# Attention and a mixture of experts in one kernel: a shorter distance for routing products, and a seventh block pair

## The chip, the cores and the metric

The kernel runs on one core of a Trainium2 chip. The metric is the device time of one execution in microseconds; the times given are a median of several runs, and beside it one execution taken by the hardware profiler. TensorE multiplies matrices, VectorE (DVE) and ScalarE (ACT) work elementwise, GpSimd (POOL) here issues the transfers that gather and scatter rows by an index, and SyncE (SP) issues plain transfers.

## The reference, cut to what matters

Channel attention over 4 batches of 5056 positions and 256 channels, and behind it a mixture of 8 experts over the 20224 rows that it gives:

```
s = normalised(k).T @ normalised(q) / tau        # 256 x 256 a batch
x = (v @ softmax(s)).reshape(20224, 256)
logits = x @ w_gate                              # 20224 x 8
# all (row, expert) pairs in falling order of their logit: a row goes to the first
# expert that still has room; each expert takes 20224 / 8 = 2528 rows
out[rows of e] = relu(x[rows of e] @ w1[e]) @ w2[e]   # 256 -> 1024 -> 256
```

The assignment depends on all logits, so the kernel finds it expert by expert: it searches the threshold above which the next full expert takes its rows, takes these rows out, and goes on with the experts that are left.

## The kernel before, in words

**Order of the work.** First attention and the gate (to about 319 us of the span), then the experts in the order in which they become full. An "expert 5" below is the one that comes sixth (p = 5). Each has 2528 rows, in chunks of up to 512 rows (`CUT`: five chunks, c = 0 to 4). A chunk is gathered from memory by row (`fetch` in `load_x`, line 1490), turned so that the 256 inputs lie on the partitions (`turn`), multiplied by w1 (`layer1`, eight groups of 128 features, six products each), and by w2 (`layer2`, one group of 24 products for each 128 rows), and scattered by row to the output (line 1753).

**Precision.** Every operand is split into a high part, rounded to the format that TensorE takes at full speed, and a low part, the difference. A product is three: high by high, high by low, low by high. ScalarE makes the high parts (copies, or relu for the hidden layer), VectorE the low ones.

**Block pairs.** `MIXED` names, for some experts, the chunks at which a pair of chunks is taken together: the first layer of both is a 2 by 2 by 2 block product, which `layers` (line 1760) forms with seven block products instead of eight. `STEPS` is its order, written out by hand: P1 to P7 are the block products, c.. and p7 copies on ScalarE, j.. joins on VectorE, hi and lo the two parts of the hidden layer. `turn_parts` prepares the chunks of a pair (with more differences and roundings than `turn`), `sums_w` the weights. Before, experts 4 and 5 have one pair (chunks 3 and 4), experts 6 and 7 two (chunks 1 and 2, 3 and 4).

**Routing.** While the experts are computed, the routing of later experts goes on in the gaps: generators (`route`, `compact`) yield the engine and the estimated cost of their next instruction, and the planner `Order` (line 1245) keeps clocks for TensorE (`pe`) and VectorE (`dve`) and puts such an instruction into the engines' queues where its inputs should be there. `hook` does this after each product of the layers. A routing product (engine "P") is put in when the end of its input, `st.ready`, lies `margin` ns behind the clock of TensorE; "q" is a product without that distance. `margin` is 0 in the first part, 150 during expert 0 (`FIRST_MARGIN`) and 700 from expert 1 on (`MARGIN`). The routing of an expert is first a search (rounds that count rows above trial thresholds: L711, L715 and ScalarE's L688, summed by a product at L860 and L873, L725 or L839), then a compaction, which makes the list of rows (products L1073, countings by ScalarE L1135, or by VectorE L1153 and L1158). For experts 6 and 7 the compaction's products, but for the first, are of kind "q" (line 1140). The list is needed when the first chunks of that expert are gathered.

**Held.** While `o.held` is set, `hook` passes over all routing streams. `layers` sets it at every step: always in a pair that begins before chunk 3, always for the last expert, and otherwise once the index list of the next expert is there.

Of the kernel before, what the change touches and what calls it, by code (L numbers as in the profile page):

```python
# [21 lines left out]
E, F = 8, 1024  # L22
# [50 lines left out]
DVE_TO_DVE = 70  # L73
EARLY_GAP = 100
MARGIN = 700
FIRST_MARGIN = 150
TURN_LAT = 1150
LAYER_LAT = 1050
# [14 lines left out]
DEPTH = 4  # L93
PAD_X = 88
PARTED = (4, 5, 6, 7)
MIXED = {4: (3,), 5: (3,), 6: (1, 3), 7: (1, 3)}
LOAD_AT = (1, 0)
GATHER_AT = {1: ("p7.0", "cAB.1", "cBZ.1", "hi12.0", "cAB.2", "p7.2", "hi11.2", "cAB.3"),
             3: ("p7.0", "cAB.1", "cBZ.1", "hi12.0", "hi21.1", "hi11.2", "cBZ.3", "hi11.3",
# [11 lines left out]
def attention_moe(ctx: ExitStack, tc: tile.TileContext, q, k, vt, tau, wg, w1t, w2t, tabs, out):  # L111
# [3 lines left out]
    P = nc.gpsimd  # L115
# [497 lines left out]
    done = {}  # L613
# [628 lines left out]
    class Order:  # L1242
        def __init__(self):
            self.pe = self.dve = self.act = 0.0
            self.margin = 0
            self.patient = self.queued = False
            self.held = self.inner = False
            self.main = []
            self.streams = []

        def add(self, gen, prio):
            st = Stream(gen, prio)
            st.mine = st.ready = max(self.dve, self.pe)
            self.streams.append(st)
            return st

        def scalar(self, at, cost):
            if not self.queued:
# [16 lines left out]
        def hook(self):  # L1275
            moved = True
            while moved:
                moved = False
                best = None
                if self.main:  # L1280
                    best = (max(self.dve, self.main[0][0]) + self.patient * GAP, 0, None)
                for st in () if self.held else list(self.streams):
                    if st.next is None:
                        self.streams.remove(st)
                        continue
                    eng, cost = st.next
                    if eng == "W":
                        st.step()
                        if st.next is None or st.next[0] != "W":
                            moved = True  # L1290
                            break
                    elif eng == "M":
                        st.mine = max(st.mine, cost)
                        st.step()
                        moved = True
                        break
                    elif eng == "A":
                        if st.ready <= self.pe:
                            st.mine = st.ready = self.scalar(self.pe, cost) + ACT_LAT
                            st.step()  # L1300
                            moved = True
                            break
                    elif eng in "Ppq":
                        if eng == "p" or st.ready + (self.margin if eng == "P" else 0) <= self.pe:
                            self.pe += cost
                            st.mine = st.ready = self.pe + PE_TO_DVE
                            st.step()
                            moved = True
                            break
                    else:  # L1310
                        c = (max(self.dve, st.mine) if eng == "V" else self.dve, st.prio(), st)
                        if self.patient and c[1] == EARLY_PRIO:
                            c = (c[0] + EARLY_GAP,) + c[1:]
                        if best is None or c[:2] < best[:2]:
                            best = c
                if moved:
                    continue
                if best is not None and best[0] <= self.pe + SLACK:
                    moved = True
                    if best[2] is None:  # L1320
                        self.run_main()
                    else:
                        st = best[2]
                        self.dve = best[0] + st.next[1]
                        st.mine = self.dve + DVE_TO_DVE
                        st.ready = self.dve + DVE_TO_PE
                        st.step()
# [13 lines left out]
    o = Order()  # L1341
# [127 lines left out]
    def load_x(p, c, paced=False):  # L1469
        idx = routed[p]["src"]  # L1470
# [19 lines left out]
        def fetch(i, col, n, after=None):  # L1490
            at = idx[:n, col:col + 1]
            if paced:
                at = ffx.tile([128, 1], I32, name="pace", bufs=4)[:n]
                S.activation(at, idx[:n, col:col + 1], AF.Copy)
            if by_v and n < 128:
                P.memset(xg[n:128, i], 0.0)
            P.memset(spacer, 0.0)
            got = P.indirect_dma_start(out=xg[:n, i, :], out_offset=None, in_=x_d,  # L1498
                                       in_offset=bass.IndirectOffsetOnAxis(ap=at, axis=0))
            if after is not None:  # L1500
                tc.add_manual_dep(got.ins, after.ins.name, SPACED, reason="room between gathers")
            if i == len(cols) - 1:
# [219 lines left out]
    def layer2(p, c, h, inserts, behind=()):  # L1722
# [4 lines left out]
        idx = routed[p]["idx"]  # L1727
        for i, col in enumerate(cols_of(p, c)):
# [7 lines left out]
            for fbs in [[fb for fb in range(8) if not any(fb in g for g in late)]] + list(late):  # L1736
                for l, w in ((hH, wH), (hH, wL), (hL, wH)) if fbs in late else ((hH, wH), (hL, wH), (hH, wL)):
                    for fb in fbs:
# [8 lines left out]
                        if j % 2 == 0:  # L1747
# [2 lines left out]
            S.activation(y[:n], py[:n, 0:C], AF.Copy)  # L1750
            o.scalar(o.pe + 200, 390)
            P.memset(spacer, 0.0)
            sd = P.indirect_dma_start(out=out, out_offset=bass.IndirectOffsetOnAxis(ap=idx[:n, col:col + 1], axis=0),  # L1753
                                      in_=y[:n], in_offset=None)
            for s_ in scat:
# [4 lines left out]
    def layers(p, c):  # L1760
# [32 lines left out]
            o.dve += 690  # L1793

        for step in STEPS:
            o.held = c < 3 or p == E - 1 or bool(done.get(("idx", p + 1)))
            op, g = step.split(".")
            g = int(g)
            A, D = fresh[g % 2], fresh[1 - g % 2]
# [40 lines left out]
    with tc.manual_schedule():  # L1840
# [62 lines left out]
        for p in range(E):  # L1903
# [80 lines left out]
            if p + 1 in PARTED:  # L1984
                at_end[0] = [cut_more]
                at = LOAD_AT[p in PARTED]
# [67 lines left out]
```

## Time and profile before

| | |
|---|---|
| median of 3 runs | 1251.32 us (1250.91 to 1252.19) |
| the profiled execution, its own time | 1249.44 us |
| its span, first to last instruction | 1247.7 us |
| TensorE busy | 1227.2 us (98%) |
| VectorE busy | 935.2 us (75%) |
| ScalarE busy | 646.6 us (52%) |
| GpSimd busy | 382.3 us (31%) |

Rows name the line of the kernel, the engine, the operation, and the tiles as output<-inputs. Times are from the start of the span, in us; a row of the order of time has start and duration, and in brackets how long the engine stood idle ahead of it and what ended that. The ends of TensorE's products are modelled, so the distance between their starts says more than their durations. The experts begin at 319 (0), 454 (1), 576 (2), 695 (3), 809 (4), 920 (5), 1033 (6) and 1138 us (7).

### The profile page before, as it was taken

To read this page: it belongs to the slowest core of one execution; us is meant where nothing else is said; L and a number is where in the kernel's file an instruction comes from. 1 tells how busy PE (TensorE), PEld (TensorE's weight loads), DVE (VectorE), ACT (ScalarE), POOL (GpSimd) and SP (SyncE) were. 2 spreads that over 40 slices of the span, in tenths; PEclk is the share of its full clock that TensorE was granted. 3 is DMA by queue.
4 is the path that set the end of the run, shared out by engine and by line. 5 is a ranking of instruction groups with operands and counts; after the bars stand their busy time and mean duration, and the time that the engine had idled before them with its cause. 6 is when DMAs were issued, how large, how long until landed. Compare 5 with 4: busy or idle time off the path is not lost.

```text
span 1247.7 us, 23699 instructions
## 1 busy us (share of the span) xinstructions
PE 1227.2 (98%) x8710; PEld 1096.5 (88%) x8710; DVE 935.2 (75%) x2396; ACT 646.6 (52%) x1491; POOL 382.3 (31%) x693
## 2 busy tenths in 40 slices
PE   8999999999999989999999999999999999999998
PEld 7889977898888978899899898988898998989898
DVE  6688597798778767877876987897787777766752
ACT  6646653467324533534542665547654565664652
POOL 0000000001532255144333434333452444444422
PEclk9999999999999999999999999999999999999999
DMA  8899875436232126344624543453454364545410
GB/s 309 308 406 415 323 267 200 157 153 257 60 88 97 49 63 162 101 111 105 168 82 94 134 116 92 111 145 95 104 141 102 101 153 114 117 103 131 106 46 33
DMA packets 223812, 184.62 MB, mean 148 GB/s; under 512 B 152656, under 2 KB 193488, under 8 KB 219088
## 3 DMA queue, kind: packets, MB, share of 16 engines
q1 hardware_dynamic: 196624, 103.66, 29.5%
q0 software_dynamic: 17664, 58.22, 14.7%
q10 hardware_dynamic: 9408, 21.24, 4.4%
q8 instruction: 68, 1.11, 0.4%
q14 instruction: 48, 0.39, 0.1%
HBM read 123.30 MB, written 59.77 MB: 147 GB/s over the span
## 4 chain that ended last, share of the span: by engine, by line
PE 82%; DMA 6%; issue 5%; POOL 2%; DVE 2%; ACT 2%; SPq 0%; POOLq 0%; ACTq 0%; DVEq 0%
PE py L1740 30%; PE ph L1691 24%; PE px L295 8%; PE s L347 8%; PE ph L1779 4%; PE py L1779 3%; DMA x_d<-xs 2%; PE pc L860 2%; DMA ua<-in_q_dram 1%; POOL out_dram L1753 1%; PE px L473 1%; DMA uc<-in_k_dram 1%; PE pi L1073 1%; POOL xg L1498 1%; DMA uc<-in_q_dram 1%
## 5 line engine op out<-in xcount | busy, mean ns | idle before, releaser
L1740 PE MATMUL py<-uc,hH 128*128 128x256 f32 (+1 forms) x2560 | 337.2, 280 | 0.5 <-ACT c L1750 0.3
L1740 PEld LDWEIGHTS py<-uc,hH 128*128 128x128 f32 (+1 forms) x2560 | 314.1, 187 | 2.9 <-ACT c L1750 0.5
L1691 PE MATMUL ph<-xH,ua 128*128 128x512 f32 (+3 forms) x928 | 251.0, 388 | 0.3 <-issue 0.2
L1498 POOL DMA_INDIRECT xg<-x_d,src x156 | 156.1, 1000 | 178.4 <-ACT hH L1694 73.4
L1694 ACT ACTIVATE hH<-ph 128x512 fp32r<-128x512 f32 (+3 forms) x232 | 134.2, 580 | 133.9 <-PE ph L1691 127.2
L1691 PEld LDWEIGHTS ph<-xH,ua 128*128 128x128 f32 x928 | 166.9, 189 | 30.4 <-ACT xH L1656 0.6
L1753 POOL DMA_INDIRECT out_dram<-y,idx x105 | 107.3, 1022 | 269.1 <-ACT y L1750 216.2
L1700 DVE SCALAR_TENSOR_TENSOR hL<-ph,hH 128x512 fp32r<-128x512 f32 (+3 forms) x232 | 153.7, 665 | 42.0 <-ACT hH L1694 36.9
L1740 PE MATMUL py<-uc,hL 128*128 128x256 f32 (+1 forms) x1280 | 181.7, 280 | 0.2 <-issue 0.2
L1740 PEld LDWEIGHTS py<-uc,hL 128*128 128x128 f32 (+1 forms) x1280 | 161.5, 187 | 0.7 <-issue 0.6
L1691 PE MATMUL ph<-xL,ua 128*128 128x512 f32 (+3 forms) x464 | 141.5, 385 | 0.0
L1750 ACT ACTIVATE y<-py 128x256 f32<-128x256 f32 (+1 forms) x105 | 40.2, 383 | 158.1 <-PE py L1740 129.1
L1691 PEld LDWEIGHTS ph<-xL,ua 128*128 128x128 f32 x464 | 85.2, 188 | 15.8
L347 PE MATMUL s<-ua 128*128 128x256 f32 x320 | 73.8, 387 | 3.3 <-DMA ua<-in_q_dram 2.3
L347 PEld LDWEIGHTS s<-ua 128*128 128x128 f32 x320 | 60.9, 193 | 15.4 <-issue 7.4
L298 ACT ACTIVATE xs<-px 128x512 f32<-128x512 f32 (+2 forms) x98 | 49.7, 520 | 47.6 <-PE px L295 45.5
L347 PE MATMUL s<-uc 128*128 128x256 f32 x320 | 71.5, 380 | 0.6 <-DMA uc<-in_q_dram 0.6
L347 PEld LDWEIGHTS s<-uc 128*128 128x128 f32 x320 | 60.2, 190 | 10.1 <-issue 1.6
L295 PE MATMUL px<-aH,vh 128*128 128x256 f32 (+1 forms) x232 | 67.7, 294 | 0.5 <-ACT aH L263 0.5
L295 PE MATMUL px<-aH,vl 128*128 128x256 f32 (+1 forms) x232 | 65.8, 284 | 1.4 <-DVE vl L274 1.4
L295 PE MATMUL px<-aL,vh 128*128 128x256 f32 (+1 forms) x232 | 65.8, 284 | 0.0
L363 DVE TENSOR_TENSOR acc_k<-acc_k,sq 128x1024 f32<-128x1024 f32 x36 | 43.9, 1220 | 19.8 <-ACT sq L362 19.3
(431 smaller groups left out, 2127.9 us busy)
## 6 DMA issues: line engine op xcount, KB each, us to landing
x_d<-xs ACTq DMA_DIRECT2D x39, 512.0 KB
xr<-xg SPq DMA_DIRECT2D x34, 512.0 KB
xq<-xr SPq DMA_DIRECT2D x136, 128.0 KB
vr<-in_vt_dram SPq DMA_DIRECT2D x14, 1024.0 KB
uc<-in_k_dram SPq DMA_DIRECT2D x18, 512.0 KB
uc<-in_q_dram SPq DMA_DIRECT2D x18, 512.0 KB
ua<-in_k_dram SPq DMA_DIRECT2D x17, 512.0 KB
ua<-in_q_dram SPq DMA_DIRECT2D x17, 512.0 KB
```

The costliest lines, as they stand in the source:

```text
L295: mm = PE.matmul(px[:, i * C:i * C + width], lhsT=l_, rhs=a_, start=(j == 0), stop=(j == len(terms) - 1))
L298: S.activation(xs[:, t % TH:t % TH + n, 0:width], px[:, 0:n * width].rearrange("p (t c) -> p t c", t=n), AF.Copy)
L347: newest[0] = PE.matmul(sb[:, ib * C:(ib + 1) * C], lhsT=kt[:, t, ib * 128:(ib + 1) * 128], rhs=qt[:, t, :], start=(first and t == 0 and i ...
L363: V.tensor_tensor(acc, acc, sq, op=OP.add)
L1498: got = P.indirect_dma_start(out=xg[:n, i, :], out_offset=None, in_=x_d, in_offset=bass.IndirectOffsetOnAxis(ap=at, axis=0))
L1691: PE.matmul(ph[:, 0:nt], lhsT=l[:, w], rhs=x_[:, kb, 0:nt], start=(i == 0), stop=(i == 5))
L1694: relu = S.activation(hH[:, fb, 0:nt], ph[:, 0:nt], AF.Relu)
L1700: V.scalar_tensor_tensor(hL[:, fb, 0:nt], ph[:, 0:nt], 0.0, hH[:, fb, 0:nt].bitcast(F32), op0=OP.max, op1=OP.subtract)
L1740: mm = PE.matmul(py[:n, 0:C], lhsT=l[:, fb, tk], rhs=w[:, d], start=(j == 0), stop=(j == 23))
L1750: S.activation(y[:n], py[:n, 0:C], AF.Copy)
L1753: sd = P.indirect_dma_start(out=out, out_offset=bass.IndirectOffsetOnAxis(ap=idx[:n, col:col + 1], axis=0), in_=y[:n], in_offset=None)
L1779: PE.matmul(dst, lhsT=w[b][l][:, f], rhs=x[a][i], start=(first and n == 0), stop=(n == 2), skip_group_check=True)
```

## The change

Three things. `MIXED` gets a second pair for expert 5, chunks 1 and 2, so that expert 5 is worked like expert 6. The planner gets a record of the row transfers: `transfer` is called at each gather and scatter with an estimated start; a transfer that would start less than 1600 ns behind the last one (each takes 1280 ns by the planner's account) marks the next 3500 ns as shaken. `room` gives the distance for routing products: `margin` while shaken, else at most 250 ns. And `o.held` is false in all pairs, so that routing goes on there.

```diff
+QUIET = 250
+POOL_STEP = 1280
+CLOSE = 1600
+SHAKEN = 3500
...
-MIXED = {4: (3,), 5: (3,), 6: (1, 3), 7: (1, 3)}
+MIXED = {4: (3,), 5: (1, 3), 6: (1, 3), 7: (1, 3)}
...
+            self.moved = self.shaken = -1e9
...
+        def transfer(self, at):
+            start = max(at, self.moved + POOL_STEP)
+            if start < self.moved + CLOSE:
+                self.shaken = start + SHAKEN
+            self.moved = start
+
+        def room(self):
+            return self.margin if self.pe < self.shaken else min(self.margin, QUIET)
...
-                        if eng == "p" or st.ready + (self.margin if eng == "P" else 0) <= self.pe:
+                        if eng == "p" or st.ready + (self.room() if eng == "P" else 0) <= self.pe:
...
+            o.transfer(o.pe + 300)
...
+            o.transfer(o.pe + 900)
...
-            o.held = c < 3 or p == E - 1 or bool(done.get(("idx", p + 1)))
+            o.held = False
```

## Rows read from the trace of the kernel before

**Rows 1.** The page: the span, and TensorE's busy time, share and instructions.

```profile
span 1247.7 us, 23699 instructions
PE 1227.2 (98%) x8710; PEld 1096.5 (88%) x8710; DVE 935.2 (75%) x2396; ACT 646.6 (52%) x1491; POOL 382.3 (31%) x693
```

**Rows 2.** Busy time of each engine (instructions), clock, DMA: experts 5 and 6.

```profile
920.10:1033.10 113.00, 111.89 (x758) 101.28 (x757) 86.72 (x221) 63.97 (x172) 46.61 (x85) 1.00 0.47 119
1033.10:1138.10 105.00, 105.00 (x702) 95.56 (x701) 72.69 (x130) 61.52 (x128) 46.42 (x83) 1.00 0.48 119
```

**Rows 3.** Waits of TensorE, 455 to 1138 us: total, times, longest.

```profile
PE pi L1073 <- ACT ext L1137: 1.1, 2, 0.9
PE pc L873 <- DVE Ex L869: 0.6, 1, 0.6
PE pc L725 <- DVE Ec L721: 0.5, 1, 0.5
PE pc L1073 <- DVE G L1064: 0.2, 1, 0.2
```

**Rows 4.** TensorE in order of time, within the pair of expert 4.

```profile
880.70 0.62 PE L1779 MATMUL py<-xH,ua 128*128 128x512 f32 x2
...
881.38 0.62 PE L1779 MATMUL py<-xH,ua 128*128 128x512 f32 x2
```

**Rows 5.** The same table as rows 2: a pair, a plain layer, a pair.

```profile
989.80:1009.20 19.40, 19.40 (x87) 15.66 (x86) 13.44 (x27) 14.49 (x26) 9.33 (x18) 1.00 0.49 116
1033.10:1044.00 10.90, 10.90 (x50) 9.04 (x49) 8.80 (x15) 8.25 (x21) 3.78 (x6) 1.00 0.50 119
...
1055.30:1074.70 19.40, 19.40 (x87) 15.65 (x86) 13.84 (x31) 14.49 (x26) 10.09 (x21) 1.00 0.48 113
```

**Rows 6.** Groups by line: a join and a copy; busy us, mean ns, idle before.

```profile
L1791 DVE TENSOR_TENSOR ph<-ph,p 128x512 f32<-128x512 f32 x24 | 16.6, 692 | 0.0
...
L1787 ACT ACTIVATE p<-py 128x512 f32<-128x512 f32 x24 | 14.4, 601 | 2.6 <-PE py L1779 2.1 <-ACT ph L1787 0.4
```

**Rows 7.** In order of time: routing products, an input of two, three transfers.

```profile
512.89 0.67 PE L860 MATMUL pc<-eq,ge 128*128 128x48 bf16 x20
...
553.37 0.95 POOL L1498 DMA_INDIRECT xg<-x_d,src  x1 [0.28 <-issue]
...
554.62 0.99 POOL L1753 DMA_INDIRECT out_dram<-c,idx  x1 [0.21 <-issue]
...
557.75 0.26 DVE L869 TENSOR_TENSOR Ex<-Dr,jsel 120x96 fp32r<-120x96 f32 x1
...
558.06 0.32 PE L873 MATMUL pc<-Ex,ones_q 128*128 128x96 f32 x1 [0.62 <-DVE Ex L869]
...
679.31 0.19 PE L873 MATMUL pc<-Ex,ones_q 128*128 128x64 f32 x1
...
795.73 0.22 PE L725 MATMUL pc<-Ec,ones_q 128*128 128x12 f32 x1
...
864.62 0.97 POOL L1753 DMA_INDIRECT out_dram<-y,idx  x1 [2.08 <-ACT y L1750]
...
865.16 0.40 DVE L836 CAST Ec<-cnt 128x8 fp32r<-128x8 f32 x1 [1.10 <-ACT junk L688]
...
865.71 0.24 PE L839 MATMUL pc<-Ec,ones_q 128*128 128x8 f32 x1
...
1022.62 0.38 PE L1073 MATMUL pc<-E__108,G 128*128 128x162 bf16 x3 [0.17 <-DVE G L1064]
```

**Rows 8.** Line 836: shortest/median/longest ns, first and last start, shapes.

```profile
L836 DVE CAST Ec<-cnt x10: 157/170/404, 854.1 to 950.2; 128x8 fp32r<-128x8 f32 x8, 128x16 fp32r<-128x16 f32 x2
```

**Rows 9.** The same for the products of lines 839 and 1073.

```profile
L839 PE MATMUL pc<-Ec,ones_q x10: 168/168/244, 854.9 to 951.4; 128*128 128x8 f32 x8, 128*128 128x16 f32 x2
...
L1073 PE MATMUL pi<-E__108,G x144: 230/233/246, 290.3 to 1044.4; 128*128 128x162 bf16 x144
```

**Rows 10.** In order of time: compaction beside the preparation of a pair.

```profile
985.34 0.40 ACT L1135 ACTIVATE junk<-pi,rhalf 128x160 bf16<-128x160 f32 x1
...
985.62 0.21 ACT L1135 ACTIVATION_READ_ACCUMULATOR junk<-pi,rhalf 128x1 f32 x1
985.71 0.18 ACT L1137 ACTIVATE ext<-pi 128x6 f32<-128x6 f32 x1
...
985.95 0.37 PE L1073 MATMUL pi<-E__108,G 128*128 128x162 bf16 x3 [0.94 <-ACT ext L1137]
```

## The prediction

> **What bounds the kernel now.** I read the page first. TensorE is busy for 1227.2 of the 1247.7 us of the span [rows 1], and the table by expert says that this is no average over unlike stages: 111.89 of 113.00 us in expert 5, 105.00 of 105.00 in expert 6, at a granted clock of 1.00, while VectorE has 86.72 and 72.69 us and ScalarE 63.97 and 61.52 us there [rows 2]. So a change is worth what it takes from, or adds to, TensorE's own stream: products fewer, or waits inside the stream. Next the waits of TensorE from expert 1 to the end of expert 6 (455 to 1138 us): 2.4 us in all, each of them a routing product (L1073, L873, L725) that stood at the head of TensorE's queue before its input was there; no row is a wait for a gathered row, a weight load or an index list [rows 3]. So nothing in this stretch waits for the routing to be finished. Routing done sooner buys no time by itself; it can only allow other things.
>
> **The sixth and seventh chunk in a block pair: a gain.** Chunks 1 and 2 of expert 5 go from two plain first layers to one block pair (the seventh pair of the kernel, there are six now). In products this is 96 against 7 x 4 x 3 = 84, so 12 fewer, of 512 columns each. Inside a pair the groups of three start 0.68 us apart (880.70, 881.38), 0.227 us a product [rows 4], so 12 x 0.227 = 2.72 us. The stages say a little less: a plain first layer without routing takes 10.90 us, two 21.80; a pair without routing 19.40, whose first products come slower [rows 5]. The difference, 2.4 us, is what I take; the 2.72 is the upper end. The second layers of both chunks are the same products as before.
>
> The Trainium skill ("TensorE: Matmul & The Clock Gate", Back-to-back issue gap) gives N/2.4 + 2.5 ns for an isolated warm product, 215.8 ns for 512 columns. An estimate by that page would be 12 x 0.2158 = 2.59 us. The trace's 0.227 us is longer and decides.
>
> What the pair adds lies on VectorE and ScalarE: 8 joins of 0.69 us and 12 copies of 0.6 us beyond the plain layers [rows 6], and a preparation with 7 more differences and 3 more roundings, by the same rows some 5 us of VectorE and 2 us of ScalarE. In expert 5 that makes about 97 of 110 us on VectorE and 74 on ScalarE. Expert 6, with the same two pairs, runs at 105.00 of 105.00 us of TensorE [rows 2], so alone this is hidden. The cover is thinner in expert 5, because routing sits there as well; that is the third part.
>
> **A shorter distance for routing products: a loss of about a microsecond.** Until now each routing product of experts 1 to 7 is put into TensorE's queue when the planner's clock is 700 ns past the planned end of its input; it becomes 250 ns unless a close transfer is noted. For expert 0 the distance is 150 already and min(150, 250) leaves it. TensorE runs its queue in order, so a product whose input is late holds every product of the layers behind it, and through them the ScalarE and VectorE work that reads those. I measured how far the input's end lies ahead of the product's start, for the 91 routing products between 455 and 1138 us for which the input can be read off. Most stand 0.7 to 1.5 us off; the floor is about 0.05 us (557.75 + 0.26 to 558.06, where TensorE waited). Whoever is under 0.50 us now would lose up to 0.45 us at the shorter distance. There are thirteen of them; the first is at 512.89, the last at 1022.62 [rows 7]. Counting a transfer as close when its row on GpSimd starts within 1.6 us of the one before, and 3.5 us behind it as shaken, 34 of the 91 are shaken, with nine of the thirteen (the transfers at 553.37 and 554.62 stand ahead of the one at 558.06), and 57 are not, with four (at 512.89, 679.31, 795.73 and 865.71) [rows 7]. So the rule of the change does pick out the risky third: 26% against 7%. The four unshaken have 0.17, 0.35, 0.17 and 0.15 us (the last from 865.16 + 0.40 to 865.71) and would lose 0.33 + 0.16 + 0.34 + 0.36 = 1.2 us. All thirteen, if the planner's guess at the transfers misses the real ones, 4.1 us. The other end is a small gain: where the routing falls elsewhere, today's waits need not return. I take +1.2, the sum over the rows to which the rule applies.
>
> The rows also show what one transfer does to a short operation: the CAST at 865.16 took 0.40 us beside a transfer that began at 864.62, where the median of its line is 170 ns and the longest of ten 404 [rows 7, 8]; that is 0.2 us more. The Trainium skill ("SBUF — State Buffer", Who interferes with whom) says that copies, casts and tensor_scalar can hold the port pair that VectorE shares with GpSimd, that whoever is second is blocked for the whole instruction, and that tensor_reduce never contends. By that rule any transfer disturbs, close or not, but by no more than its own length, and 250 ns would cover the 0.2 us seen; the shorter distance would then cost nothing. The four unshaken steps, 0.8 us and more short of the usual distance, say that something else is late there as well (ScalarE's counting ahead of the CAST, 1.10 us of idle time). The rule is the ground of the first rival below.
>
> **Routing in pairs: about half a microsecond lost.** Today the routing streams stand still in every first pair, in all of expert 7, and in the second pair once the next index list is there. The stages at 989.80 and 1055.30 have 13.44 and 13.84 us of VectorE and 14.49 of ScalarE in 19.40 [rows 5], so 5 to 6 us of either are free. A search round of routing 6 (ten of them, 854.9 to 951.4 [rows 9]) brings 3 countings of 0.6 us on ScalarE, a compaction of 6 or 7 twelve more. The planner keeps account of VectorE, but not of ScalarE. The bounds: nothing, as at 1055.30, where the last index work on VectorE lay in the pair's start and the pair still took 19.40 us [rows 5]; and 0.94 us for each group of compaction products that meets the preparation of a block pair, as at 985.95, where ext was released late because ScalarE had the pair's roundings between the countings [rows 10]. The groups behind the first carry no distance at all (L1140). With routing earlier by some 15 us (about 55 searching steps by 0.45, a third of them shaken) and no longer stopped at 878, both compactions slide from the second layers of expert 5 toward its pairs. The waits at 985.95 and 1022.62, 1.3 us together with the smaller one [rows 3], leave their places; I take two of 0.94 in their stead, so +0.6.
>
> **Sum.** -2.4 + 1.2 + 0.6 = -0.6 us. The profiled execution took 1249.44 us (span 1247.7), so 1248.8; the median of the runs is 1251.32, so I forecast 1250.7. A measurement of this kernel can tell about 0.2%, 2.5 us, from no change.
>
> **Rivals.**
> 1. The distance was mostly idle cover, and the late compaction leaves without coming back. For it: 57 of 91 products stand unshaken and only four of these under 0.50 us, and the delay by one transfer is 0.2 us, under 250 ns. Against it: the four unshaken ones, which no close transfer made late. Time: -2.4 - 1.3 = -3.7, 1247.6.
> 2. Slower: ScalarE becomes the bound inside the pairs. The two compactions have four groups of three countings on ScalarE each, and products that go out without distance. A pair leaves ScalarE 4.9 us, and twelve countings with their readings take 12 x 0.6 = 7.2. If a compaction runs within a pair, each group's product waits as the one at 985.95 did. With seven groups at 0.94: -2.4 + 1.2 - 1.3 + 6.6 = +4.1, 1255.4. It decides from six groups on. Against it: today 13 groups beside second layers brought one such wait, and the spill of a pair ends in the second layer, where ScalarE is half idle.
> 3. The notes of transfers miss the real ones (the planner puts them at fixed offsets from its own clock), and all thirteen pay: -2.4 + 4.1 + 0.6 = +2.3, 1253.6.
> A change that doesn't do what it says would be one where nearly all steps stay shaken; that gives the pair alone, 1248.9, and belongs between the forecast and the first rival.
>
> **How the numbers follow.** Forecast 0.40 (its own range 1249 to 1252.5), first rival and the pair alone 0.37, second 0.15, third 0.08. Faster by over 0.2% (under 1248.8): nearly all of the first rival and a little of the forecast, 0.38. Slower by over 0.2% (over 1253.8): the second and half of the third, 0.19. Within: 0.43. The range leaves a tenth on either side: from 1246.5, just under the first rival, to 1254.8, inside the second.
>
> **What would show it.** 84 more block products (504 now, six pairs of 84) and 96 fewer plain ones. The new pair's stage at 19.4 to 20 us, and expert 5 at about 111 us instead of 113.00; over 113 means that pairs carry the price. TensorE's waits on routing products between expert 1 and the end of expert 6: 2.4 now; 3 to 5 by the forecast, under 2 by the first rival, over 8 by the second, with L1073 behind ACT ext inside a pair as its longest row. The last routing product, at 1044.4 now [rows 9], earlier by 15 us or more; if it is not, the distance was seldom shortened. The forecast is wrong if experts 1 to 4, where no pair changes, move by more than 2 us in sum.

## The result, and the profile after

The changed kernel took 1257.69 us (1255.97 to 1259.87), the kernel before in the same runs 1251.32: a ratio of 1.0055 [1.0043, 1.0067]. I had forecast 1250.7 with 0.19 for slower by over 0.2%. It is slower, by 6.4 us, where my sum said -0.6. In another group of runs the ratio was 1.0031 [1.0018, 1.0043] (+4.4 us by the medians).

The profiled execution took 1257.69 us. First the page: span, then busy time and instructions by engine.

```profile
span 1255.9 us, 23717 instructions
PE 1231.0 (98%) x8698; PEld 1091.9 (87%) x8698; DVE 940.7 (75%) x2411; ACT 651.2 (52%) x1506; POOL 381.2 (30%) x693
```

TensorE has 12 instructions fewer than in [rows 1], the twelve products that I counted, so the change does what it says. The span grew by 8.2 us all the same. The table by expert says where. Columns as in [rows 2]; these are experts 3 to 6 of the kernel after.

```profile
697.80:812.20 114.40, 112.90 (x751) 102.03 (x749) 98.49 (x284) 67.22 (x210) 44.26 (x81) 1.00 0.46 114
812.20:926.30 114.10, 112.20 (x743) 99.52 (x742) 92.75 (x247) 72.08 (x215) 47.21 (x84) 1.00 0.48 118
926.30:1040.30 114.00, 112.02 (x745) 96.99 (x744) 90.30 (x222) 67.49 (x170) 46.64 (x85) 1.00 0.46 117
1040.30:1145.90 105.60, 105.12 (x699) 95.43 (x698) 68.76 (x110) 58.60 (x112) 45.88 (x83) 1.00 0.49 120
```

Expert 5 has 13 instructions of TensorE fewer than in [rows 2] and takes 1.0 us longer, not 2 less. Against before, experts 0 to 7 differ by -0.4, +1.3, +2.2, +0.9, +2.6, +1.0, +0.6 and +0.4 us. (Unchanged stretches differ by up to 0.9 us from trace to trace; the length of expert 1 varied by 2.2 us, 121.4 to 123.7, among kernels in which nothing of it is changed.) Expert 4 has lost most, and the products of its layers are the same.

Of these differences not all come back. In a second trace of the changed kernel, set against one of the kernel before, both from groups in which the kernel before takes 1240 us, experts 2 to 5 differ by +0.7, +0.2, +2.7 and -0.2 us, and experts 0, 1, 6 and 7 by 0.1 at most. Expert 4 is what both pairs of traces show.

The waits of TensorE, 455 to 1150 us, in the columns of [rows 3]:

```profile
PE py L1755 <- ACT c L1765: 1.5, 2, 1.0
PE pc L729 <- DVE Ec L725: 1.5, 3, 0.6
PE pc L843 <- DVE Ec L840: 1.4, 4, 0.5
PE py L1795 <- ACT p L1803: 0.5, 1, 0.5
PE pc L877 <- DVE Ex L873: 0.5, 2, 0.3
PE ph L1795 <- ACT ph L1803: 0.5, 2, 0.3
PE ph L1795 <- DVE c L1807: 0.3, 1, 0.3
PE pc L864 <- issue: 0.3, 1, 0.3
```

Two kinds are here. Routing products wait on their inputs (L729, L843, L877), as the shorter distance allows. The other kind is new: the layers' own products wait (L1755, L1795), behind ScalarE's copies and VectorE's joins. All but one of them stand in the pairs of experts 4 and 5 and in the second layer ahead of the new pair. The waits of routing products sum to 3.7 us, inside the 3 to 5 that I had forecast; the 2.8 us of the layers' own products had no place in the forecast. The compaction product L1077 behind ACT ext, which I had named as the longest row of my second rival, is not among them.

Next the stages, cut at their first product. "Routing" is the number of routing products in the stage.

| stage | before: us, routing | after: us, routing |
|---|---|---|
| expert 4, pair | 19.34, 0 | 21.87, 3 |
| expert 5, up to the second layers of chunks 1, 2 | 44.70, 7 | 45.41, 20 |
| expert 5, second layers of 1, 2 | 25.06, 22 | 22.46, 7 |
| expert 5, pair of 3, 4 | 19.36, 0 | 23.54, 20 |
| expert 5, second layers of 3, 4 | 23.95, 19 | 22.61, 0 |

The routing has moved from the second layers into the pairs. The second layers give back 2.6 and 1.3 us; the pair of 3 and 4 pays 4.2. The second line holds the new pair: two plain first layers against one pair should have made it 2.4 us shorter, and it is 0.7 longer. Its parts after, from the table by stage (second layer of chunk 0, then the new pair; the third row is that second layer in the second trace):

```profile
937.60:950.00 12.40, 11.37 (x98) 11.09 (x97) 9.45 (x19) 5.09 (x10) 3.51 (x5) 1.00 0.28 54
950.00:971.70 21.70, 21.58 (x104) 15.79 (x103) 19.09 (x52) 17.37 (x47) 11.26 (x22) 1.00 0.61 156
...
929.10:940.50 11.40, 11.40 (x98) 11.21 (x97) 9.52 (x19) 5.09 (x10) 3.62 (x5) 1.00 0.20 42
```

Against 11.22 us for the same second layer before and 19.40 for a pair without routing [rows 5]. VectorE is at 19.09 of 21.7 us and ScalarE at 17.37. The layer ahead of the new pair is thus 1.2 us longer in one trace (12.42 us) and 0.2 in the other (11.38); the new pair takes 21.74 us in both.

What a pair with routing looks like, in order of time (pair of expert 4, after; in brackets the idle time ahead and what ended it):

```profile
883.37 0.17 DVE L840 CAST Ec<-cnt 128x16 fp32r<-128x16 f32 x1
883.70 0.25 PE L843 MATMUL pc<-Ec,ones_q 128*128 128x16 f32 x1 [0.52 <-DVE Ec L840]
...
891.50 0.42 ACT L692 ACTIVATE junk<-Gf,bias 128x160 bf16<-128x160 f32 x1
...
892.32 0.41 ACT L692 ACTIVATE junk<-Gf,bias 128x160 bf16<-128x160 f32 x1
...
892.73 0.58 ACT L1803 ACTIVATE p<-py 128x512 f32<-128x512 f32 x1
...
893.37 0.74 PE L1795 MATMUL py<-xH,ua 128*128 128x512 f32 x2 [0.55 <-ACT p L1803]
```

First a search product stands at the head of TensorE's queue 0.52 us before its input is there. Then three countings of a search round, 0.41 us each, stand in ScalarE's queue ahead of the copy that empties a result of the pair, and TensorE waits 0.55 us for that result's place. Both come from the search rounds to which the three routing products of this pair belong.

Such waits are not the whole. The three pairs of experts 4 and 5 take 67.1 us for 58.1 without routing, 9.1 more. By the spacing of the starts on TensorE, 2.4 of these are the 41 routing products themselves (0.06 us each), 2.1 the waits that the profile lists, and 4.6 layers' products that start later than in a pair without routing, with no listed wait ahead of them. The new pair has no listed wait at all. That the routing work on ScalarE and VectorE delays these products as well is likely, and not shown.

The routing did end earlier, as forecast. The search's and the compaction's products, columns as in [rows 9]:

```profile
L843 PE MATMUL pc<-Ec,ones_q x10: 168/244/277, 847.6 to 927.0; 128*128 128x8 f32 x8, 128*128 128x16 f32 x2
...
L1077 PE MATMUL pi<-E__108,G x144: 230/233/244, 289.7 to 1007.9; 128*128 128x162 bf16 x144
```

The last one starts at 1007.9, 36 us before the 1044.4 of [rows 9].

### The profile page after: what moved, and what is told of

Same layout as the page of the kernel before. It is cut to its first block, busy times and chain, and to the rows that moved or that the text cites. A ratio compares the mean times of both kernels' runs of the same rounds, so it can differ in the third digit from the quotient of the medians.

```text
span 1255.9 us, 23717 instructions
## 1 busy us (share of the span) xinstructions
PE 1231.0 (98%) x8698; PEld 1091.9 (87%) x8698; DVE 940.7 (75%) x2411; ACT 651.2 (52%) x1506; POOL 381.2 (30%) x693
## 4 chain that ended last, share of the span: by engine, by line
PE 70%; issue 12%; DMA 6%; POOL 5%; DVE 3%; ACT 2%; SPq 1%; POOLq 0%; ACTq 0%; DVEq 0%
PE py L1755 24%; PE ph L1706 19%; PE s L351 8%; PE px L299 8%; PE ph L1795 3%; PE py L1795 3%; POOL out_dram L1769 3%; DMA x_d<-xs 2%; PE pc L864 2%; POOL xg L1512 2%; DMA ua<-in_q_dram 1%; PE px L477 1%; DMA uc<-in_k_dram 1%; PE pi L1077 1%; DMA xq<-xr 1%
## 5 line engine op out<-in xcount | busy, mean ns | idle before, releaser
L1755 PE MATMUL py<-uc,hH 128*128 128x256 f32 (+1 forms) x2560 | 337.3, 279 | 2.1 <-ACT c L1765 2.1
L1755 PEld LDWEIGHTS py<-uc,hH 128*128 128x128 f32 (+1 forms) x2560 | 313.8, 187 | 5.1 <-ACT c L1765 2.7
L1706 PE MATMUL ph<-xH,ua 128*128 128x512 f32 (+3 forms) x864 | 235.4, 389 | 0.5 <-ACT xH L1671 0.4
L1709 ACT ACTIVATE hH<-ph 128x512 fp32r<-128x512 f32 (+3 forms) x216 | 124.4, 578 | 120.1 <-PE ph L1706 109.4
L1755 PE MATMUL py<-uc,hL 128*128 128x256 f32 (+1 forms) x1280 | 179.6, 279 | 0.2
L1706 PEld LDWEIGHTS ph<-xH,ua 128*128 128x128 f32 x864 | 155.3, 189 | 27.9 <-ACT xH L1671 1.1
L1715 DVE SCALAR_TENSOR_TENSOR hL<-ph,hH 128x512 fp32r<-128x512 f32 (+3 forms) x216 | 142.5, 662 | 43.9 <-ACT hH L1709 40.3
L1755 PEld LDWEIGHTS py<-uc,hL 128*128 128x128 f32 (+1 forms) x1280 | 160.7, 187 | 0.7 <-issue 0.5
L1706 PE MATMUL ph<-xL,ua 128*128 128x512 f32 (+3 forms) x432 | 132.4, 385 | 0.0
L1706 PEld LDWEIGHTS ph<-xL,ua 128*128 128x128 f32 x432 | 79.7, 189 | 14.7
L1139 ACT ACTIVATE junk<-pi,rhalf 128x160 bf16<-128x160 f32 x124 | 48.2, 393 | 20.7 <-PE pi L1077 14.7
```

Source lines behind the costliest of these rows:

```text
L1139: S.activation(junk, pi[:, i * W:i * W + COLS], AF.Sign, bias=rhalf[:, g0 + i:g0 + i + 1], scale=-1.0, accum_out=sgn[:, g0 + i:g0 + i + 1])
L1706: PE.matmul(ph[:, 0:nt], lhsT=l[:, w], rhs=x_[:, kb, 0:nt], start=(i == 0), stop=(i == 5))
L1709: relu = S.activation(hH[:, fb, 0:nt], ph[:, 0:nt], AF.Relu)
L1715: V.scalar_tensor_tensor(hL[:, fb, 0:nt], ph[:, 0:nt], 0.0, hH[:, fb, 0:nt].bitcast(F32), op0=OP.max, op1=OP.subtract)
L1755: mm = PE.matmul(py[:n, 0:C], lhsT=l[:, fb, tk], rhs=w[:, d], start=(j == 0), stop=(j == 23))
```

## The experiments

Each kernel was compared with the kernel before in the runs of its own group. The kernel before took 1250.97, 1239.99, 1239.83, 1239.59 and 1248.67 us in the five groups, so only ratios are carried from group to group.

### Each part alone, and the pair with the distance

```diff
# e1, in the kernel before
-MIXED = {4: (3,), 5: (3,), 6: (1, 3), 7: (1, 3)}
+MIXED = {4: (3,), 5: (1, 3), 6: (1, 3), 7: (1, 3)}
# e2, in the changed kernel: the old MIXED and the old line of o.held
# e3, in the kernel before
-            o.held = c < 3 or p == E - 1 or bool(done.get(("idx", p + 1)))
+            o.held = False
# e4, in the changed kernel
-            o.held = False
+            o.held = c < 3 or p == E - 1 or bool(done.get(("idx", p + 1)))
```

> The seventh pair alone, with the old distance and the old holding of the routing. If the pair itself is sound (my theory): 2 to 3 us under before, its stage at 19.4 us, as in the first pair of experts 6 and 7. If the pair is what costs (rival: its preparation and the output tiles of its expert, the 1.03 us wait on ACT c in the second layer ahead of it): 0 to 2 us over before. If the held routing now comes late: a wait of several us ahead of expert 6.

> The shorter distance alone; pairs and holding as before. In the changed kernel experts 1 to 3, which have no pair, are 4.4 us longer in sum (1.3, 2.2, 0.9). If that is the distance: 3 to 5 us over before, with these three experts longer by the same 4.4. If the distance is harmless and those stages moved for another reason: within 1 us of before.

> Routing goes on in all pairs, with the long distance and the six pairs of before. If routing inside pairs costs by itself (ScalarE's countings and VectorE's index work ahead of the pair's own copies): each pair that holds routing takes 21.5 us or more instead of 19.4, 2 to 6 us over before. If it costs only behind a short distance: within 1 us of before, pairs at 19.4 to 20.

> The changed kernel with the routing held in pairs as before: seven pairs and the shorter distance. If most of the loss lies inside the pairs: 3 to 5 us under the changed kernel, so 1 to 3 us over before (the pair's 2.4 against the 4.4 of experts 1 to 3). If the distance is the whole loss: no better than the changed kernel, 6 us over before.

Measured: the pair alone 1.0377 [1.0354, 1.0400] (1296.86 us, 46 us over), the distance alone 1.0065 [1.0051, 1.0079], routing in pairs alone 1.0032 [1.0021, 1.0042] (+4.1 us), pair and distance 1.0256 [1.0239, 1.0272].

The pair alone costs 46 us, which no line of the prediction allowed for. Its experts 4 to 6:

```profile
810.00:920.90 110.90, 110.76 (x742) 100.14 (x741) 90.25 (x249) 66.57 (x184) 47.00 (x85) 1.00 0.47 121
920.90:1064.80 143.90, 116.61 (x746) 103.14 (x744) 96.87 (x235) 73.41 (x193) 45.68 (x81) 0.91 0.34 89
1064.80:1185.40 120.60, 110.44 (x699) 99.65 (x700) 74.41 (x132) 61.71 (x124) 46.91 (x85) 0.94 0.46 110
```

Expert 5 is 30.9 us longer than before and TensorE idle for 27 of its 143.9. The end of it, in order of time, is the start of expert 6:

```profile
1047.43 1.00 POOL L1498 DMA_INDIRECT xg<-x_d,src  x1 [1.65 <-DVE src L1203]
...
1054.35 0.38 SPq L1483 DMA_DIRECT2D xr<-xg  x1
...
1063.42 1.32 DVE L1619 STREAM_TRANSPOSE ph<-xq 128x512 f32<-128x512 f32 x2 [8.26 <-DMA xq<-xr]
...
1064.18 1.19 ACT L1625 ACTIVATE xH<-ph 128x512 fp32r<-128x512 f32 x2 [7.84 <-DVE ph L1619]
...
1064.83 1.39 PE L1691 MATMUL ph<-xH,ua 128*128 128x512 f32 x2 [9.45 <-ACT xH L1625]
```

The first rows of expert 6 are gathered at 1047.43, right behind the last step of its index (`src`), which stands at 1047.0; in the kernel before that step stands at 989.8 and this gather at 992.3, in the changed kernel the step at 983.8. VectorE, ScalarE and TensorE stand for the rows, TensorE 9.45 us. The routing stands still in a pair; a second held pair takes 19.4 us of gap from the search of expert 6, whose ten rounds (L839) now run from 855.7 to 989.1, where before they ended at 951.4 [rows 9]. After the change they run from 847.6 to 927.0. So the three parts are no sum: the seventh pair needs the other two (the table below has all combinations).

The distance alone moved experts 2 and 3 by +2.0 and +1.2 us, and expert 5 by +6.8, where compaction products now stood early (TensorE's waits in expert 5 of that kernel, columns as in [rows 3]):

```profile
PE pi L1077 <- ACT ext L1141: 3.3, 2, 2.5
PE pc L1059 <- DVE cb L1053: 1.0, 1, 1.0
PE pc L1077 <- issue: 0.9, 1, 0.9
PE pc L1077 <- DVE G L1068: 0.6, 1, 0.6
```

The longest of these, behind ext, is the wait of my second rival, though in a second layer and not in a pair. Routing in pairs alone moved expert 4 by +1.9 and expert 5 by +1.9: the pair of expert 4 took 21.38 us with a single routing product in it.

### The other pairs of parts, and the guard for close transfers

```diff
# e5, in the changed kernel
-QUIET = 250
+QUIET = 700
# e6, in the changed kernel: the old MIXED
# e7, in the kernel before with the new MIXED: routing in the pairs of expert 5 alone
-            o.held = c < 3 or p == E - 1 or bool(done.get(("idx", p + 1)))
+            o.held = c < 3 and p != 5 or p == E - 1 or bool(done.get(("idx", p + 1)))
# e8, in the changed kernel with the old MIXED and the old line of o.held: no guard
-SHAKEN = 3500
+SHAKEN = -5000
```

> Seventh pair and routing in all pairs, long distance throughout. The two runs so far: the pair alone, with routing held, 46 us over before (routing late), routing in pairs alone 4 us over. If letting the routing run is what makes the pair possible (my theory): the 40 us of waiting are gone, and the loss is that of the pairs, 4.1 - 2.4 + about 2.4 for the seventh pair's own routing, so 2 to 6 us over before. If the shorter distance is needed as well to have the lists in time (rival): 10 us or more over before, with a wait of TensorE ahead of expert 6.

> Shorter distance and routing in pairs, six pairs. Against the changed kernel this lacks only the seventh pair. If the pair's 12 products saved are eaten by the routing inside it: within 1.5 us of the changed kernel, 5 to 8 us over before. If the pair itself gains its 2.4 us there: 8 to 10 us over before. If it costs: under 5 us over before.

> Seventh pair, long distance, routing held in pairs as before, but not in the new pair itself (and the second of expert 5, where the old rule lets it go until the list of expert 6 is there). By my theory the 40 us of late routing shrink to nothing or nearly, the pair of expert 4 is back at 19.4 us, and only expert 5's pairs carry routing: -2.4 + 2 to 4, so 0 to 2 us over before. If the stop in the pair of expert 4 (19 us) is what makes the routing late: 10 us or more over before.

> As the run with the shorter distance alone, but 250 ns behind close transfers too. If the products behind close transfers are the risky ones (26% against 7% of them under 0.50 us before): 2 to 4 us over that run, 10 to 13 us over before. If the note of close transfers picks nothing out: as that run, 8 us over before.

Measured: e5 1.0226 [1.0211, 1.0241], e6 1.0034 [1.0022, 1.0047], e7 1.0246 [1.0233, 1.0259], e8 1.0102 [1.0088, 1.0116]. With the first four, ratios of all eight combinations:

| | neither | distance | routing in pairs | both |
|---|---|---|---|---|
| six pairs | 1 | 1.0065 | 1.0032 | 1.0034 |
| seven pairs | 1.0377 | 1.0256 | 1.0226 | 1.0055, 1.0031 |

Nothing beats the kernel before. The pair adds 3.8% alone, 1.9% with either part, and between 0 and 0.2% with both. In e5 and e7 I had expected 2 to 6 and 0 to 2 us over before, and it is 28 and 31: routing in pairs is not enough by itself to have the lists in time. It costs 0.3%; on top of it the distance costs nothing that can be measured (1.0032 to 1.0034). In the trace of e6 expert 5 takes 111.8 us, with none of the waits for which e2 paid 6.8 us there; no run separates the two.

On the guard: experts 1 to 3 took 354.8 us in e6 (with it) and 354.8 in e8 (without it), 353.5 in e5 and e7. It buys nothing there, against my 26% to 7%. The Trainium skill ("SBUF — State Buffer", Who interferes with whom), says that where VectorE and GpSimd contend for the port pair that they share, the one that comes second is blocked for the whole instruction; by that a close transfer disturbs no more than another, and these lengths agree. Most of what e8 loses is one wait of 7.4 us of a compaction product on VectorE in expert 5, a matter of where it fell, and expert 4 is 1.3 us longer than in e7, with 20 routing products in its first stage for 3; for experts 4 and 5 the comparison settles nothing. The price of the shorter distance in experts 2 and 3 depends on the group: +3.1 us in the first trace of the kernel after and +3.2 in e2, from groups where the kernel before takes 1251 us; +1.2 in e6 and +0.9 in the second trace of the kernel after, from groups where it takes 1240.

### The changed kernel again, with one kind of routing kept out

```diff
# e9, in the changed kernel: the compaction of experts 6 and 7 waits within pairs
-            o.held = False
+            o.held, o.inner = False, True
...
-        o.held = False
+        o.held = o.inner = False
# e10, in the changed kernel: routing stands still in the pair of expert 4
-            o.held = False
+            o.held = p == 4
# e11, in the changed kernel: the long distance up to expert 3
-            return self.margin if self.pe < self.shaken else min(self.margin, QUIET)
+            return self.margin if self.pe < self.shaken or not self.late else min(self.margin, QUIET)
...
+            o.late = p > 3
```

> The changed kernel again, beside the three that follow: 5 to 7 us over before, as measured.

> The changed kernel, but the compactions of experts 6 and 7 stand still within pairs (the search goes on there). In its trace the pairs of expert 5 take 21.74 and 23.54 us with 18 and 20 compaction products in them. If ScalarE's countings and VectorE's index work ahead of the pair's copies are the cause (my theory): these pairs at 19.4 to 20.5, the products at some 0.1 us each in the second layers, expert 5 about 3 us shorter. If the products cost the same anywhere (rival): expert 5 within 1 us of the changed kernel. If the lists then come late: expert 5 or 6 longer by 5 us or more.

> The changed kernel with routing held in the pair of expert 4 alone. That pair back at 19.4 us, so 2.2 to 2.6 us off expert 4. If the 19 us of routing given up there were spare: 2 us under the changed kernel in all. If they are what keeps the lists of experts 6 and 7 in time: experts 5 and 6 longer by 5 us or more, as in the runs with the seventh pair and the routing held.

> The changed kernel with the long distance up to the end of expert 3, the short one from expert 4 on. Experts 1 to 3 back at the lengths of before (1 to 4 us less). If the routing that the short distance brings forward there (some 10 us) is needed for the seventh pair: a wait at the end of expert 5, 10 us or more over the changed kernel, near the run with the seventh pair, routing in pairs and the long distance (27 us over before). If not: 1 to 4 us under the changed kernel.

Measured: the changed kernel 1.0031 [1.0018, 1.0043], e9 1.0044 [1.0025, 1.0063], e10 1.0030 [1.0018, 1.0043], e11 1.0028 [1.0013, 1.0042]: all alike. By stage, the changed kernel in these runs: the pair of expert 4, the two of expert 5, the second layers behind, and the whole of expert 5. Behind it e9: the last pair of expert 5, the second layers behind it, the whole.

```profile
873.60:895.50 21.90, 20.66 (x90) 15.73 (x89) 17.93 (x44) 17.04 (x43) 9.37 (x18) 1.00 0.37 92
940.50:962.20 21.70, 21.58 (x104) 15.75 (x103) 19.01 (x51) 17.41 (x47) 11.15 (x22) 1.00 0.62 156
985.40:1009.00 23.60, 22.80 (x107) 16.07 (x106) 17.67 (x46) 18.52 (x54) 9.38 (x18) 1.00 0.41 90
1009.00:1030.80 21.80, 21.80 (x193) 21.80 (x192) 15.53 (x25) 9.96 (x21) 11.37 (x20) 1.00 0.54 151
...
917.90:1030.80 112.90, 111.98 (x745) 97.14 (x744) 89.85 (x220) 67.08 (x168) 46.61 (x84) 1.00 0.46 117
```

```profile
983.00:1003.00 20.00, 20.00 (x93) 15.88 (x92) 14.14 (x23) 15.23 (x33) 9.32 (x18) 1.00 0.36 94
1003.00:1029.30 26.30, 23.34 (x207) 23.05 (x206) 19.86 (x46) 14.09 (x42) 11.88 (x21) 1.00 0.59 139
...
915.00:1029.30 114.30, 110.18 (x745) 98.89 (x744) 90.80 (x219) 68.65 (x168) 47.33 (x84) 1.00 0.47 117
```

e9 brings the pair from 23.6 to 20.0 us, so compaction is what made it long; but the second layers take 26.3 instead of 21.80, and expert 5 is 1.4 longer (1.0 of it in the layer ahead of the new pair, 12.35 us here). I had expected 3 us back, and that was wrong. e10 does the same a step ahead, in expert 4; its pair and the last pair of expert 5:

```profile
872.80:892.10 19.30, 19.30 (x85) 15.57 (x85) 13.27 (x21) 14.49 (x26) 9.29 (x17) 1.00 0.48 113
981.40:1007.30 25.90, 23.80 (x112) 17.33 (x111) 18.03 (x49) 18.84 (x57) 8.03 (x15) 0.93 0.34 92
```

The pair of expert 4 is back at 19.3 (21.9 with three routing products), expert 4 at 111.2 instead of 113.6, and expert 5 takes 115.0 instead of 112.9. e11 takes 0.7 us from expert 2 and has expert 5 at 116.0. Wherever the routing of experts 6 and 7 is kept out, it costs as much where it goes. TensorE's largest wait in expert 5 names the place, of e9 (in the second layers of chunks 3 and 4) and of e10 (in the pair ahead of them; e11 has the same with 2.1):

```profile
PE pi L1077 <- ACT ext L1141: 3.0, 2, 2.2
```

```profile
PE pc L1059 <- DVE cb L1053: 2.1, 1, 2.1
```

In e9 it is once more the wait of the second rival, outside the pairs. In e10 and e11 the granted clock fell to 0.50, the lower of its two levels, just behind that wait (at 989.7 and 991.0), and for a while the pair's products start 0.43 us apart and not 0.23.

### Without the routing of experts 6 and 7

```diff
# e12, in the kernel before: no search and no compaction for experts 6 and 7
+        if p >= E - 2:
+            while not done.get(("out", p - 1)):
+                yield "W", 0
+            routed[p] = dict(routed[p - 1])
+            done["ei", p] = done["idx", p] = done["out", p] = True
+            return
# e13, as e12 with the new MIXED: seven pairs
# e16, as e13, the turn of chunk 2 one group of rows later in the second layer of chunk 0
# e17, the same in the changed kernel
-TURN_B = 0
+TURN_B = 1
```

e12, e13 and e16 use the rows and weights of expert 5 for experts 6 and 7, so they leave out what these two should compute.

> The kernel before, for its lengths by expert on this chip: by theory as on the first chip but for expert 0, with expert 5 at 112 to 113 us.

> The kernel before (six pairs), with the search and compaction of experts 6 and 7 left out: these take the rows and weights of expert 5 again, so their outputs are not the reference's, but gathers, layers and scatters are the same in number and size. Expert 5 without routing should be a pair's saving above the 105.0 us of expert 6: 107.4 us. This run is the base for the next.

> The same with the seventh pair. If the pair is sound and only the routing beside it takes its gain (my theory now, after the run without compaction in pairs showed the cost moving and not going): 2.4 us under the run with six pairs, expert 5 at 105.0 us. If the pair costs by itself in expert 5, by its preparation and output tiles (rival): as the run with six pairs, or over it.

> The run with seven pairs and the routing of experts 6 and 7 left out, but chunk 2 (of experts 5, 6 and 7) is turned behind the first 128 rows of the second layer ahead of it, not before them. In the run without this its rows landed late (2.36 us of VectorE's idle time behind xq<-xr), and ScalarE's output copies stood behind its roundings: second layer 13.75 us instead of 10.92. If that is what ate the pair's gain: this second layer at 11 to 12 us, expert 5 at 105 to 106, 2 us under the run with six pairs. If the copies are late all the same: 13 us or more, and nothing gained; if the pair now waits for its chunk: its stage over 20 us.

> The changed kernel with the same edit. By theory 0 to 1.5 us under the changed kernel (its second layer ahead of the new pair had one wait of 1.0 us on the first chip and none on another), so still 2 to 5 us over before: the routing in the pairs of experts 4 and 5 stays.

Measured: the kernel before against itself 1.0004 [0.9993, 1.0014], six pairs 0.9961 [0.9948, 0.9974] (so the late routing costs the kernel before 4 to 5 us), seven pairs 0.9967 [0.9955, 0.9978], seven with the later turn 0.9957 [0.9941, 0.9972], the changed kernel with it 1.0043 [1.0027, 1.0059]. Even with no routing in its way the seventh pair gains nothing that the times can tell (0.9967 for 0.9961), though expert 5 is 0.9 us shorter in the trace. Expert 5 with six pairs (first row), then with seven: the whole, the second layer of chunk 0, the new pair.

```profile
911.20:1019.50 108.30, 107.56 (x711) 97.91 (x710) 59.66 (x95) 50.87 (x97) 46.21 (x84) 1.00 0.47 116
```

```profile
911.10:1018.50 107.40, 105.40 (x698) 95.49 (x698) 68.82 (x110) 58.82 (x112) 47.03 (x84) 1.00 0.48 118
922.00:935.70 13.70, 11.70 (x97) 11.20 (x96) 8.63 (x14) 4.98 (x10) 4.18 (x7) 1.00 0.47 124
935.70:955.10 19.40, 19.40 (x86) 15.67 (x86) 12.28 (x19) 14.48 (x26) 10.11 (x21) 1.00 0.48 115
```

The pair is the 19.40 us that I took. The layer ahead of it takes 13.75 us instead of 10.92, more than the 2.4 that the pair saves; that expert 5 still ends sooner is due to the second layers behind the pair (21.80 for 23.01). Within the layer ahead, in order of time:

```profile
927.00 1.30 DVE L1552 STREAM_TRANSPOSE xg<-xq 128x512 f32<-128x512 f32 x2 [2.36 <-DMA xq<-xr]
928.40 0.63 ACT L1562 ACTIVATE xH<-xg 128x512 fp32r<-128x512 f32 x1 [5.09 <-DVE xg L1552]
928.93 0.36 ACT L1756 ACTIVATE p<-py 128x256 f32<-128x256 f32 x1
...
929.35 1.19 PE L1746 MATMUL py<-uc,hH 128*128 128x256 f32 x8 [1.45 <-ACT p L1756]
```

A pair needs both its chunks turned before it starts, so the rows of chunk 2 are due about a first layer (11 us) sooner than in plain order. They land late: VectorE waits 2.36 us for them, ScalarE stands 5.09 us behind VectorE with its rounding, and the copy that gives TensorE its place stands behind the rounding. In the kernel after the same row shows 1.06 us at 941.28 and TensorE's longest wait, 1.03 us at 947.14; in its second trace VectorE does not wait there, TensorE has no wait, and the layer takes 11.38 us. e16 should have given the rows time; the layer still took 14.1 us, with VectorE now idle 4.2 us ahead of that row (its wait put down to the scatter of a result). So that the late rows are the cause is read from these rows and not shown by an experiment; an earlier gather was not tried. With routing in place, e17's layer took 11.40 us, as the second trace did without the edit.

## Why the prediction was wrong

The counts held: twelve products fewer, a clean pair of 19.40 us, routing done 36 us sooner. The step that failed is the third, routing in pairs, priced at +0.6; alone it measures 1.0032, +4.1 us (e3). With it fell the argument ahead of the sum, by which the three parts could be priced each by itself.

1. **"Nothing in this stretch waits for the routing to be finished."** True of the kernel before and false as a step of the argument: the waits show what is late now, not how much room there is. With one more held pair the list of expert 6 comes 57 us later (1047.0 for 989.8) and costs 46 us (e1). The distance and the routing in pairs were not two edits beside the pair; they are what it needs, and my sum of three terms could not show that.
2. **Routing in pairs, +0.6, measured +4.1.** I priced one mechanism, a compaction product behind ext, and took its number of waits from the kernel before. In the changed kernel's pairs that wait does not occur (it does in the second layers of e2 and e9). What the traces show there is another: countings stand in ScalarE's queue ahead of the pair's copies, and TensorE waits for a result's place. The pair of expert 4 went from 19.34 to 21.87 us with three routing products, in both traces. In expert 5 the two pairs take 6.6 us more than pairs without routing and the second layers give back 3.9, again in both. How much of this is ScalarE's queue is not shown: the listed waits are 2.1 of the 9.1 us in the three pairs. I had the row for it, 14.49 of 19.40 us on ScalarE [rows 5], and read the 4.9 left over as room. In a queue that runs in order the order counts: what is needed soonest stands behind what came first.
3. **The seventh pair, -2.4, measured about 0.** The pair itself was right. I named expert 6 as cover, where the same two pairs run at 105.00 of 105.00; but expert 6 has next to no routing beside it. In the second trace of the changed kernel expert 5 up to its second layers takes 44.30 us, for 44.71 in the kernel before; without the 2.4 us by which routing lengthens the new pair, the saving is there, and routing in the pairs, net 2.6 us in expert 5, takes it. The layer ahead of the pair was left out as well: it loses 1.2 us in the first trace, 0.2 in the second, and without routing 2.8 (e13).
4. **The distance, +1.2.** Right in size for experts 2 and 3 where the kernel before takes 1240 us (+1.2 in e6, +0.9 in the second trace), too low where it takes 1251 (+3.1 and, in e2, +3.2). I counted the products that stand close now. With a shorter distance the routing also falls elsewhere, and products with ample distance before get into places where their input is late: the 6.8 us of expert 5 in e2.
5. **The rivals.** The second gave 1255.4, nearest to the measured time; it had the right engine and the wrong wait, and its condition (six groups waiting in pairs) was not met, so that its time is near is in part luck. Expert 5 stands at 114.0, over the 113.00 that I gave as the sign that pairs carry the price (at 112.9 in the second trace), and experts 1 to 4 moved by +7.0 us in sum (+3.7 there), of which 2.6 is expert 4 with its pair: the sign that I gave for a wrong forecast.

By place, the +8.2 us of the two spans is +4.4 in experts 1 to 3 (distance, with 1.3 in expert 1 that lies within what varies), +2.6 in expert 4 (search in its pair), +1.0 in expert 5 (compaction in its pairs, less what the second layers give back, and the layer ahead of the new pair against its gain), +0.2 in the rest. A small slip of the sum on ScalarE (63.97 + 7.2 + 2 is 73, not 74) changes nothing.

What remains open: whether earlier gathers of chunk 2 would let the seventh pair gain its 2.4 us, why those rows are late in some traces and not in others, and what delays the pairs' products where the profile lists no wait.

## What to carry to other kernels

A stream that runs in the gaps of another needs gaps enough before its deadline: ahead of taking a gap away, compare the end of the stream with the time at which its result is first read, and not with the waits of now. Where an engine works through its queue in order, as ScalarE does in the rows above, free time is no room: look for what the next engine needs soonest, and count what is put ahead of it. A cheaper block brings forward the time at which all its inputs must be there; price the stage ahead of it too.

## What was not expected of the hardware

In e1 the two products behind the wait of 9.45 us take 1.39 us where two of the same shape take 0.62 [rows 4]. The granted clock had fallen to 0.50, the lower of its two levels (1.2 for 2.4 GHz), at 1048.4, when TensorE had just stood idle for 4.09 us, and rose to 1.00 at 1068.9, with TensorE at work without a listed wait since 1064.83:

```profile
1048.40:1068.90 20.50, 7.60 (x28) 5.01 (x28) 8.37 (x19) 5.70 (x24) 7.93 (x17) 0.50 0.75 154
```

So a stretch with long waits costs twice: the waits, and products at half the clock beside and behind them.

The kernel before took 1251 us beside the result and in one group of runs, 1249 in another and 1240 in three. The traces put most of the difference into one place: expert 0 takes 134.8 us in the trace beside the result and 127.5 in one from a group with 1240, while experts 1 to 7 agree within 0.9 us each. In the longer one search products wait for VectorE in expert 0, 4.1 us in sum, and in the other TensorE has no wait there. Expert 0 has the short distance of 150 already. What makes the inputs late in some groups is not shown; the distance of 250, too, cost 3 us in experts 2 and 3 where the kernel before takes 1251 us, and 1 where it takes 1240.
